# Inverting a 64x64 triangular block on 32x32 diagonal blocks: a DeltaNet and MLP kernel on one core

## The chip, the cores and the metric

The kernel runs on one core of one Trainium2 chip. The metric is the time of one execution on the device in microseconds (us). A core has TensorE (PE: matmuls; PEld: their weight loads, as many as matmuls: 7,158 of each on the page of the kernel before), VectorE (DVE), ScalarE (ACT), GpSimd (POOL) and SyncE (SP, which here only issues DMA transfers). Runs that were marked slow are named as such and left out of the ratios.

## The reference

32 independent heads (4 batches of 8) of 768 steps with head size 48 go through a recurrent "delta rule"; the 8 heads of a batch side by side are the 384 inputs of a two-layer MLP with a tanh-GELU.

```python
k_n = k / (norm(k) + 1e-06)
for t in range(S):                       # S = 768
    y[t]  = q[t] @ state                 # state is 48 x 48 per head
    v_old = k_n[t] @ state
    state = state + beta[t] * outer(k_n[t], v[t] - v_old)
x = y as rows of 384 (8 heads x 48)
h = x @ w_in                             # 384 x 2048
out = gelu_tanh(h) @ w_out               # 2048 x 384
```

The kernel takes 64 steps at a time (a chunk; 12 of them). Inside a chunk the recurrence is a triangular system: with N the masked, beta-scaled product K K^T (64x64 per head), it needs the inverse of I + N. Once that inverse is there, a chunk is a handful of small matmuls per head, and only the state goes from chunk to chunk.

## The kernel before

Every operation is recorded with a cost, the names it reads and writes and a priority; a scheduler in the kernel file then puts them into a fixed order for each engine. So the order that runs is not the order of the source. Heads are handled in pairs: `a` is the head of the pair (upper or lower 64 partitions), `p` the pair (16), `g` half of the pairs (8). The inverse is a Newton iteration on the whole 64x64 block, five rounds of two products and two evictions (copies out of PSUM, where the products of this kernel are written):

```python
def prod(hx, lhs, rhs):                      # 16 matmuls of 64x64x64
    def body():
        return [(bank(hx)[64 * a:64 * a + 64, 64 * p:64 * p + 64], lhs[64 * a:64 * a + 64, p, :],
                 rhs[64 * a:64 * a + 64, p, :], True, True, True) for p in range(8) for a in range(2)]
    return f_mms(body)
...
op(mm_pe(16, 64), {"pe": tr_w}, ...)         # W = I + N transposed on TensorE, 16 transposes
op({"act": 0.6}, {"act": f_act(X[:, :, :], bankb)}, ...)
for j in range(5):
    op(mm_pe(16, 64), {"pe": prod(h1, Zo, X)}, ...)
    op(d_ps(512), {"dve": f_tt(F[:, :, :], bc(twoI), v1(h1), ALU.subtract)}, ...)   # F = 2I - Z'X
    op(mm_pe(16, 64), {"pe": prod(h2, F, Zo)}, ...)
    op(d_act(512), {"act": f_act(dst, v1(h2))}, ...)                                # next Z
```

K and Q are transposed by a DMA transpose per chunk (`KQT`). A chunk's outputs come out with time on the partitions (`x`), and a second DMA transpose (`xT`) turns them for the MLP:

```python
op({"sp": 1.1}, {"sp": f_dma(KQT[i]..., KQ[i]..., True)}, ...)                  # per chunk
op({"sp": 1.1}, {"sp": f_dma(xT[:, s, :, 0:n], x[0:n, s, :, :]..., True)}, ...) # per MLP tile
```

## Time and profile before

| | before |
|---|---|
| median of the first three runs | 323.46 us (323.24 to 327.57) |
| span of the profiled run | 322.0 us |
| TensorE busy | 272.2 us, 85% |
| TensorE waits marked "issue" | 12.7 us |
| instruction packets | 56 of 16 KB |

These lines are from the page of the kernel before: busy us (share of the span) and number of instructions of each engine; busy tenths of TensorE in 40 equal slices and the clock granted to it in tenths; and the DMA queue that carries instructions (packets, MB, share of the engines' span).

```profile
PE 272.2 (85%) x7158; PEld 178.4 (55%) x7158; DVE 175.0 (54%) x279; ACT 175.3 (54%) x309; POOL 127.1 (39%) x96
...
PE   1158745988859789999899979989999999989995
...
PEclk9998775779998799999999999999999999999999
...
q8 instruction: 56, 0.92, 1.2%
```

TensorE is the bound from the 15th slice on. This line of the wait view of the kernel before says how long TensorE stood with nothing to wait for that the profile shows ("issue"): total us, number of times, longest.

```profile
PE ps L301 <- issue: 12.7, 12, 4.0
```

The two MLP layers' matmuls are these groups of the kernel before (count, then busy us and mean ns of one, then idle us before them):

```profile
L301 PE MATMUL ps<-xT,W 128*128 128x512 bf16 (+1 forms) x336 | 80.6, 364 | 1.8 <-ACT gT L294 1.0 <-DMA xT<-x 0.7
L301 PE MATMUL ps<-W,gT 128*128 128x384 bf16 x384 | 70.0, 327 | 0.6 <-ACT gT L294 0.6
```

And this is the timeline of TensorE in the middle of the kernel before: start us, us, form, count.

```profile
128.10 0.44 PE L301 MATMUL ps<-Z,F 64*64 64x64 bf16 x16
128.38 0.67 PE L301 MATMUL ps<-X,Z 64*64 64x64 bf16 x32
128.98 0.82 PE L301 MATMUL ps<-xT,W 128*128 128x512 bf16 x3
```

### The profile page before, as it was taken

To read this page: it belongs to the slowest core of one execution; us is meant where nothing else is said; L and a number is where in the kernel's file an instruction comes from. 1 tells how busy PE (TensorE), PEld (TensorE's weight loads), DVE (VectorE), ACT (ScalarE), POOL (GpSimd) and SP (SyncE) were. 2 spreads that over 40 slices of the span, in tenths; PEclk is the share of its full clock that TensorE was granted. 3 is DMA by queue.
4 is the path that set the end of the run, shared out by engine and by line. 5 is a ranking of instruction groups with operands and counts; after the bars stand their busy time and mean duration, and the time that the engine had idled before them with its cause. 6 is when DMAs were issued, how large, how long until landed. Compare 5 with 4: busy or idle time off the path is not lost.

```text
span 322.0 us, 15234 instructions
## 1 busy us (share of the span) xinstructions
PE 272.2 (85%) x7158; PEld 178.4 (55%) x7158; DVE 175.0 (54%) x279; ACT 175.3 (54%) x309; POOL 127.1 (39%) x96
## 2 busy tenths in 40 slices
PE   1158745988859789999899979989999999989995
PEld 1147644656636466666556556555566556544662
DVE  3489723767557467766775566674556554320111
ACT  4325543668447578634778443777345774168330
POOL 2842330877987257455546371260202211000000
PEclk9998775779998799999999999999999999999999
DMA  7998889879998435495557541709001002101022
GB/s 134 168 182 169 131 119 180 155 151 172 170 176 139 93 69 102 85 181 111 111 100 107 113 103 51 118 4 118 26 29 53 2 9 48 66 36 24 24 75 49
DMA packets 116206, 31.84 MB, mean 99 GB/s; under 512 B 110640, under 2 KB 115760, under 8 KB 116144
## 3 DMA queue, kind: packets, MB, share of 16 engines
q1 hardware_dynamic: 113600, 27.73, 45.5%
q0 software_dynamic: 2544, 3.15, 6.8%
q8 instruction: 56, 0.92, 1.2%
q14 instruction: 6, 0.05, 0.0%
HBM read 20.64 MB, written 4.72 MB: 79 GB/s over the span
## 4 chain that ended last, share of the span: by engine, by line
PE 51%; DMA 22%; issue 7%; DVE 7%; ACT 5%; SPq 4%; POOL 2%; POOLq 0%
PE ps L301 50%; DMA kf<-in_k_dram 8%; DMA qf<-in_q_dram 6%; DMA vf<-in_v_dram 4%; SPq L309 4%; DMA xT<-x 2%; DVE F L285 2%; DMA KQT<-KQ 1%; ACT Z L294 1%; ACT sq L294 1%; ACT x L294 1%; PE ps L600 1%; POOL sr L285 1%; DVE ss L503 1%; DVE R L285 1%
## 5 line engine op out<-in xcount | busy, mean ns | idle before, releaser
L285 DVE TENSOR_TENSOR F<-twoI,ps 128x512 bf16<-128x512 bf16 x120 | 80.4, 684 | 58.4 <-PE ps L301 57.7
L301 PE MATMUL ps<-xT,W 128*128 128x512 bf16 (+1 forms) x336 | 80.6, 364 | 1.8 <-ACT gT L294 1.0
L294 ACT ACTIVATE Z<-ps 128x512 bf16<-128x512 f32 x96 | 56.2, 595 | 42.3 <-PE ps L301 41.5
L294 ACT ACTIVATE gT<-ps 128x512 bf16<-128x512 f32 (+1 forms) x112 | 58.2, 536 | 32.3 <-PE ps L301 31.2
L301 PE MATMUL ps<-W,gT 128*128 128x384 bf16 x384 | 70.0, 327 | 0.6 <-ACT gT L294 0.6
L301 PE MATMUL ps<-X,Z 64*64 64x64 bf16 x1920 | 53.9, 201 | 12.8 <-ACT Z L294 6.9
L301 PE MATMUL ps<-Z,F 64*64 64x64 bf16 x1920 | 54.7, 201 | 8.7 <-DVE F L285 4.0
L301 PEld LDWEIGHTS ps<-X,Z 64*64 64x64 bf16 x1920 | 42.8, 116 | 29.8 <-ACT Z L294 15.1
L301 PEld LDWEIGHTS ps<-Z,F 64*64 64x64 bf16 x1920 | 43.0, 115 | 28.7 <-DVE F L285 15.8
L285 POOL TENSOR_TENSOR W<-identB,N 128x512 bf16<-128x512 bf16 x20 | 23.0, 1151 | 81.8 <-DVE N L285 78.1
L301 PEld LDWEIGHTS ps<-W,gT 128*128 128x128 bf16 x384 | 34.5, 98 | 21.8 <-ACT gT L294 0.8
L301 PEld LDWEIGHTS ps<-xT,W 128*128 128x128 bf16 x336 | 26.7, 100 | 23.1 <-ACT gT L294 4.2
L290 DVE COPY osb<-ps 128x384 f32<-128x384 f32 x20 | 11.1, 557 | 41.3 <-PE ps L301 41.3
L285 POOL TENSOR_TENSOR sr<-ss,half 128x16 f32<-128x16 f32 x9 | 26.2, 2911 | 5.4 <-DVE ss L503 5.2
L285 POOL TENSOR_TENSOR KQ<-kf,rn 128x768 bf16<-128x768 f32 (+1 forms) x12 | 17.1, 1423 | 21.2 <-PE ps L301 16.9
L285 POOL TENSOR_TENSOR NU<-mU,bcol 128x1024 f32<-128x1024 f32 x12 | 23.6, 1971 | 4.4 <-DVE N L285 4.0
L294 ACT ACTIVATE x<-ps 64x768 bf16<-64x768 f32 x24 | 19.3, 804 | 8.2 <-PE ps L301 7.9
L285 POOL TENSOR_TENSOR Z<-identB,N 128x512 bf16<-128x512 bf16 x20 | 23.0, 1151 | 0.0
L294 ACT ACTIVATE TT<-ps 128x512 bf16<-128x512 f32 x24 | 14.3, 596 | 13.4 <-PE ps L301 13.4
L294 ACT ACTIVATE X<-ps 128x512 bf16<-128x512 bf16 x24 | 14.3, 595 | 12.9 <-PE ps L600 12.9
L285 DVE TENSOR_TENSOR N<-ps,NU 128x512 bf16<-128x512 f32 x24 | 16.3, 686 | 8.6 <-PE ps L301 8.6
L301 PE MATMUL ps<-KQT 48*64 48x128 bf16 x384 | 12.7, 246 | 6.6 <-DMA KQT<-KQ 6.4
(49 smaller groups left out, 202.4 us busy)
## 6 DMA issues: line engine op xcount, KB each, us to landing
kf<-in_k_dram SPq DMA_DIRECT2D x24, 192.0 KB, 4.0
qf<-in_q_dram SPq DMA_DIRECT2D x24, 192.0 KB, 3.9
vf<-in_v_dram SPq DMA_DIRECT2D x24, 192.0 KB, 4.3
out_dram<-osb SPq DMA_DIRECT2D x20, 192.0 KB, 1.9
W<-in_moe_w_in_dram POOLq DMA_DIRECT2D x3, 512.0 KB, 6.0
W<-in_moe_w_out_dram POOLq DMA_DIRECT2D x4, 384.0 KB, 7.1
out_dram<-osb SPq DMA_DIRECT2D x8, 96.0 KB, 2.7
BL<-in_beta_dram SPq DMA_DIRECT2D x2, 96.0 KB, 3.6
```

Source lines behind the costliest of these rows:

```text
L285: return lambda e: e.tensor_tensor(out() if callable(out) else out, a() if callable(a) else a, b() if callable(b) else b, op)
L290: return lambda e: e.tensor_copy(out, a() if callable(a) else a)
L294: return lambda e: e.activation(out, a() if callable(a) else a, func)
L301: ins = t.matmul(out, lhsT, rhs, start=st, stop=sp_, skip_group_check=skip)
L309: return lambda e: e.dma_start(out, a)
L503: op({"dve": 0.95 * w}, {"dve": lambda e, u=u: e.tensor_reduce(ss[j][:, u], sq[j][:, u, :], AX.X, ALU.add)}, reads=[f"sq{j}{n}"], writes=[ ...
L600: ins = t.transpose(bankb()[r, p, :], W[r, p, :], identB[r, :])
```

## The change

The intent: only the two 32x32 diagonal blocks of each 64x64 block are inverted by Newton, which takes four rounds, not five, and 32 columns per product, not 64; one merge step then makes the off-diagonal block. The evictions get half as wide. In numbers of matmuls per chunk: 8 products of 64 matmuls of 32x32, and 96 for the merge, in place of 20 products of 16 and 32 transposes. Five more things are in the same change: W is no longer transposed on TensorE (VectorE transposes N); the Gram products (K K^T and Q K^T of a chunk) are cut into smaller matmuls; the outputs are made with time along the free dimension, so the MLP needs no DMA transpose, but six small SBUF-to-SBUF copies per tile and weights loaded in row groups; K and Q of the first three chunks are transposed on TensorE; and the scheduler keeps TensorE on MLP products for 1.2 us at a time.

```diff
-            for j in range(5):
-                op(mm_pe(16, 64), {"pe": prod(h1, Zo, X)}, ...)
-                ...
+            def prod(h, lhs, rhs):                       # 64 matmuls of 32x32x32
+                    for n, p in enumerate(range(ps_.start, ps_.stop)):
+                        for b in BLK:                    # four blocks of 32 partitions
+                            r.append((bank(h)[b, 32 * n:32 * n + 32], lhs(b, p), rhs(b, p), True, True, True))
+            for st in range(4):
+                op(cp, {"pe": prod(h1, cmp_(src), cmp_(X))}, mode="n", ...)
+                op(d_ps(w), {"dve": f_tt(F..., bc(twoI, n_p), view(h1), ALU.subtract)}, ...)
+                op(cp, {"pe": prod(h2, cmp_(F), cmp_(src))}, mode="n", ...)
+                ...
+            op(..., {"pe": f_mms(hm)}, mode="t", ...)    # merge: 32 matmuls
+            op(..., {"pe": f_mms(tm)}, mode="t", ...)    # merge: 64 matmuls
... (Gram products: 48 matmuls per half, in place of 16)
-            op({"sp": 1.1}, {"sp": f_dma(xT[:, s, :, 0:n], x[0:n, s, :, :]..., True)}, ...)
+            for c_ in range(2):
+                for j in range(KT):
+                    op({"sp": 0.5}, {"sp": f_dma(xs[64 * c_ + 48:64 * c_ + 64, j, :, 0:n], xs[...])}, ...)
... (K/Q transposes of chunks 0 to 2 on TensorE)
+                    if e == "pe" and pe_mode == "m" and o.mode != "m" and burst < BURST:   # BURST = 1.2
+                        pr += 5000.0
```

In all TensorE has 11,043 matmuls in place of 7,155; each is two instructions, the weight load and the matmul. (The pages count 11,046 and 7,158, three more each.)

## The prediction

> **What bounds the kernel now.** The profile's page shows TensorE busy 272 of 322 us (85%); VectorE and ScalarE are at 54%, GpSimd 39%. From about 120 us (busy time in 20 us windows) TensorE is busy 18.2 to 19.9 of every 20 us at full clock: it is the bound. Before that it idles 39 us, the DMA engines are about 90% busy to 100 us, and the granted clock falls to 0.59 between 40 and 60 us.
>
> **TensorE now (timeline and group views, from 130 us).** A 64x64 product on two diagonal tiles starts every 17.6 ns, so a batch of 16 takes 0.28 us; products on four tiles start every 8.3 ns. A chunk spends 20x0.28 on Newton, 2x0.28 on transposing W, 0.7 on the Gram products, 1.9 on the state: 8.7 us, 105 us over 12 chunks. The MLP needs about 124 us (0.216 us per 512-column matmul, 0.1625 per 384). Each change between MLP and small products costs 95 ns more than the normal spacing (309 against 216 ns, 125 against 28); the instruction order has 224: 21 us.[...]
>
> **After.** Per chunk: 8 products of 64 32x32 matmuls. Not in this trace; if four tiles start together every ~26 ns (the four-tile groups here show 31 at 48 columns), one is ~0.42 us. Merge ~1.0, Gram 0.8, state 1.65 (the output product now uses four tiles): 6.9 us, 83 us in all. So TensorE saves only ~22 us of work, though VectorE's F evictions fall from 80 to ~33 us, ScalarE loses ~40, GpSimd ~25; mostly off the critical path. PE transposes of chunks 0 to 2 add ~3 us. MLP/small changes fall to 134 (-8.6 us)[...].
>
> **Early phase.** The first Gram waits for the DMA transpose (10.2 to 15.0 us in the chain): on TensorE plus an eviction about 2.5 us sooner. The transpose also holds SyncE's queue 3 to 5 us each; the first MLP tile's transpose is only issued at 49.3 and lands at 56.8 us. Six small copies instead (0.6 us issue each) should start the MLP at 42 to 46 us. I count ~13 us less idle, ~4 us less cold clock.
>
> **New cost.** TensorE instructions grow from 7,155 to 11,043 matmuls. The wait view already has 12.7 us of TensorE "issue" waits. Instruction packets in the trace are 16 KB, ~1.1 us each.[...] Fetch may limit dense stretches: I add ~4 us, perhaps 15.
>
> **Sum.** -22 -8.6 +3 +3.6 (work) -13 -4 (early) +4 (fetch) ≈ -37, on 323.5: about 285 us. Range 269 to 300. Chances: faster by over 2% 0.96, within 2% 0.03, slower 0.01.
>
> **Right if:** 32x32 batches of 64 span ~0.42 us between batch starts; TensorE busy ~235-245 us and still the bound after 100 us; first MLP matmul before 47 us; F evictions ~33 us; idle before 120 us near 25 us.
>
> **Wrong if:** the 32x32 matmuls don't overlap four-fold; "issue" waits on TensorE exceed 25 us; the new serial chain (full-width steps, not two interleaved halves) leaves TensorE waiting on evictions after 120 us; the row-split first-layer weights land later than the first tile is ready; or the early phase gains much more than counted (then under 270).

The sum is -22 -8.6 +3 +3.6 -13 -4 +4 = -37.0 us. The ~26 ns under "After" is an estimate from the 31 ns that stand beside it, and so is the ~0.42 us made of it; the other times of new work there are estimates too, for which the text gives no working. The 4 us of fetch is an estimate beside the 12.7 us of issue waits and the 1.1 us of a packet; how it follows from them is not said. The "3 to 5 us" of SyncE are 3.2 to 4.7 us for the six transposes issued up to 80.2 us, and 1.2 to 4.7 us for all 19.

## More of the kernel before

The start times of the 56 instruction packets are in the trace. The four shortest distances from one to the next are 3.30, 3.62, 3.66 and 3.68 us; none is shorter. The packets are of 16 KB each and take 0.88 to 1.81 us, and the 56 of them go with 14,316 TensorE instructions (7,158 weight loads and 7,158 matmuls): 256 for each packet.

## The result, and the profile after

The changed kernel takes 416.96 us (412.89 to 419.55, 4 runs, one of them slow); the kernel before, 325.27 us in the same rounds. The ratio is 1.278 (95% interval 1.265 to 1.291): 28% slower, where 12% faster was predicted. A ratio here and below is the mean time of one kernel's fast runs over that of the other's of the same rounds, so it is not quite the ratio of the medians.

The same lines of the page, of the changed kernel:

```profile
PE 298.8 (72%) x11046; PEld 190.1 (46%) x11046; DVE 143.4 (34%) x250; ACT 137.5 (33%) x229; POOL 106.0 (25%) x82
...
PE   1336446996475596888886679779655497999996
...
PEclk9999997559557668599866885989765569999999
...
q8 instruction: 86, 1.41, 1.4%
```

VectorE, ScalarE and GpSimd did get lighter, as intended. TensorE has 27 us more busy time and 118 us in which it is not busy, in place of 50. The wait view of the changed kernel names the reason for most of that:

```profile
PE ps L311 <- issue: 86.6, 49, 4.4
```

It is 74 us more than before. And the MLP matmuls, whose number and size did not change, take 21.7 us longer (172.3 in place of 150.6), by the groups of the changed kernel:

```profile
L311 PE MATMUL ps<-x,W 128*128 128x512 bf16 (+1 forms) x336 | 89.3, 414 | 4.4 <-DMA x<-x 2.5
L311 PE MATMUL ps<-W,gT 128*128 128x384 bf16 x384 | 83.0, 372 | 1.8 <-issue 1.8
```

What an issue wait looks like is best seen in the chain that ended last. This is a stretch of it in the changed kernel: start us, us, what (count of matmuls).

```profile
316.35 2.46 issue
318.81 1.26 PE ps L311 x101
320.08 2.32 issue
322.40 1.24 PE ps L311 x121
323.64 2.23 issue
325.87 1.95 PE ps L311 x117
327.82 1.62 issue
329.44 1.40 PE ps L311 x114
330.84 2.35 issue
```

A sawtooth: 1.2 to 2 us of matmuls, then 1.6 to 2.5 us of nothing, with a period of about 3.6 us. Most counts are a little under 128 (the chain view puts a few matmuls on other steps). Counting all TensorE instructions in the trace, weight loads too, between the ends of these stalls gives 256 almost everywhere: the stalls from 305 to 331 us begin at the instructions 17857, 18113, 18625, 18881, 19137, 19393 and 19649. All differences are 256 or 512. A packet of the instruction queue starts 0.1 to 0.7 us before each of these stalls (for example at 308.74, 316.12, 319.93 and 323.52 us) and TensorE goes on 1.3 to 1.5 us after it has landed. In the whole trace all 49 issue waits begin at such a place, and so do 11 of the 12 in the kernel before, whose Newton matmuls are 64x64: the stalls go with the count of instructions, and not with 32x32 tiles as such.

So the reading is: instructions come in blocks of 256 (a packet of 16 KB for each, so 64 bytes per instruction), and in the train above a block is entered 3.5 to 3.8 us after the one before it (for example at 318.81, 322.40, 325.87, 329.44 and 333.19 us). A Newton product of 64 matmuls is 128 instructions and about half a microsecond of work (7.5 to 8.5 ns per matmul in this trace), so a block of such products is used up in a little over 1 us.

The second loss goes with the first. In this train of stalls TensorE's granted clock falls to half (0.50 from 320 to 340 us). These are two lines of the changed kernel's timeline,

```profile
94.62 1.47 PE L311 MATMUL ps<-W,gT 128*128 128x384 bf16 x8
...
311.61 2.74 PE L311 MATMUL ps<-W,gT 128*128 128x384 bf16 x8
```

where eight such matmuls take 1.47 us after 6.7 us without a stall (at 94.62 us) and 2.74 us in the train of stalls (at 311.61 us). From one of these matmuls to the next it is 163 ns at 94.62 us and 320 ns at 311.61 us. By the clock records of the two traces, half clock was granted for 157 us of the span in the changed kernel and for 36 us before; one stretch of it, 34 us long, starts at 307.2 us and covers the rest of this train, in which stalls of about 2.3 us have about 1.2 us of small matmuls between them.

### The profile page after: what moved, and what is told of

Its sections match the earlier page's. It is cut to its first block, busy times and chain, and to the rows that moved or that the text cites. A ratio compares the mean times of both kernels' runs of the same rounds, so it can differ in the third digit from the quotient of the medians.

```text
span 416.6 us, 22911 instructions
## 1 busy us (share of the span) xinstructions
PE 298.8 (72%) x11046; PEld 190.1 (46%) x11046; DVE 143.4 (34%) x250; ACT 137.5 (33%) x229; POOL 106.0 (25%) x82
## 4 chain that ended last, share of the span: by engine, by line
PE 68%; issue 20%; DVE 5%; SPq 2%; ACT 2%; DMA 2%
PE ps L311 66%; SPq L319 2%; PE ps L599 1%; DMA x<-x 1%; DMA BL<-in_beta_dram 1%; DVE F L295 1%; DVE DT L653 1%; ACT Z L304 1%; DVE X L295 1%; ACT TT L304 1%; DVE U L295 0%; DVE KQ L295 0%; DVE NT L667 0%; DVE KQT L300 0%; DVE N L295 0%
## 5 line engine op out<-in xcount | busy, mean ns | idle before, releaser
L311 PE MATMUL ps<-x,W 128*128 128x512 bf16 (+1 forms) x336 | 89.3, 414 | 4.4 <-DMA x<-x 2.5
L311 PE MATMUL ps<-Z,F 32*32 32x32 bf16 x2688 | 34.7, 183 | 32.5 <-issue 27.8
L295 DVE TENSOR_TENSOR F<-twoI,ps 128x512 bf16<-128x512 bf16 (+1 forms) x39 | 25.0, 645 | 76.7 <-PE ps L311 76.6
L311 PEld LDWEIGHTS ps<-x,W 128*128 128x128 bf16 x336 | 32.2, 110 | 41.1 <-issue 12.4
L304 ACT ACTIVATE Z<-ps 128x512 bf16<-128x512 f32 (+1 forms) x39 | 21.9, 564 | 79.7 <-PE ps L311 79.6
L311 PEld LDWEIGHTS ps<-Z,F 32*32 32x32 bf16 x2688 | 28.7, 94 | 38.2 <-issue 31.4
L311 PE MATMUL ps<-X,Z 32*32 32x32 bf16 x2304 | 26.5, 183 | 25.8 <-issue 24.2
L311 PEld LDWEIGHTS ps<-X,Z 32*32 32x32 bf16 x2304 | 21.5, 94 | 33.0 <-issue 26.9
L295 POOL TENSOR_TENSOR NU<-mN,bcol 128x1024 f32<-128x1024 f32 x12 | 23.1, 1929 | 11.8 <-DVE N L295 11.6
L311 PE MATMUL ps<-KQT 48*32 48x64 bf16 (+1 forms) x1152 | 16.3, 233 | 13.6 <-issue 10.9
```

Of the source, the lines that this page charges most:

```text
L295: return lambda e: e.tensor_tensor(out() if callable(out) else out, a() if callable(a) else a, b() if callable(b) else b, op)
L304: return lambda e: e.activation(out, a() if callable(a) else a, func)
L311: ins = t.matmul(out, lhsT, rhs, start=st, stop=sp_, skip_group_check=skip)
```

## The experiments

The theory, A: the supply of instructions. Its rivals: B, one of the other parts of the change (transposed outputs, copies, weight loads, ordering) costs the time; C, the serial chain of full-width evictions, or the changes between tile shapes (95 ns each between MLP and small products, by the prediction's reading of the trace; the expectations call this time drains), holds TensorE, and "issue" is only how that shows.

### 1. The old inverse in the changed kernel

```diff
-                gram(c, g)
-            if c == 0: inverse(c, slice(0, 8), "a"); inverse(c, slice(8, 16), "b")
-            else:      inverse(c, slice(0, NP), "w")
+                intra(c, g)          # 64x64 Newton and Gram products of the kernel before
```

> The changed kernel with the old 64x64 Newton inverse and old Gram products put back; everything else of the change stays. Theory A (instruction supply[...]): 7,203 matmuls again, 57 blocks, TensorE issue waits back under 20 us, time 300 to 320 us. Rival B (the transposed outputs, the six small copies, the split weight loads or the new ordering cost the time): stays above 380 us.

(The trace of the changed kernel: the shortest distance between packet starts there is 3.24 us.)

It takes 321.53 us (320.15 to 324.12); the kernel before, 325.61 us. Ratio 0.988 (0.979 to 0.996). The wait view of this run:

```profile
PE ps L311 <- issue: 7.6, 30, 1.8
```

and of its page:

```profile
q8 instruction: 56, 0.92, 1.2%
```

All of the loss goes with the inverse; rival B falls. It also shows that everything else in the change together is worth about 1.2%, not the 6 to 7% that the prediction gave to it (-8.6 +3 -13 -4, about -23 us; some 4 us less for this kernel, whose order has 172 changes between MLP and small products and not 134).

### 2. The new inverse alone

The kernel before with only masks, Gram products and inverse taken from the changed one.

> The kernel before with only its inverse and Gram products exchanged for the new 32x32 ones; transposes, outputs, weight loads and ordering rules as before. Theory A: 10,995 matmuls, about 86 blocks, TensorE issue waits of 70 to 110 us in a train of 256-instruction steps, time 390 to 430 us. Rival B: 300 to 330 us.

It takes 438.63 us, ratio 1.347 (1.338 to 1.355). Of its wait view:

```profile
PE ps L301 <- issue: 94.6, 60, 5.2
```

and of its page:

```profile
q8 instruction: 86, 1.41, 1.4%
```

The inverse does it alone. That it is even slower than the whole change (1.278) suggests that the other parts help more when TensorE is being starved; which of them was not followed up.

### 3. Half of the Newton matmuls left out

```diff
                     for n, p in enumerate(range(ps_.start, ps_.stop)):
+                        if p % 2:
+                            continue
                         for b in BLK:
```

The result is wrong. All evictions, dependences and tile shapes are as in the changed kernel.

> The changed kernel with every second matmul of the eight Newton products left out (wrong result on purpose); evictions, their sizes, the order of dependences and the tile shapes stay. It has 7,971 matmuls, about 62 blocks. Theory A: issue waits under 30 us, time 310 to 345 us, though the left-out array work is only about 20 us. Rival C (the serial chain of full-width evictions, or drains between tile shapes, holds TensorE): 395 us or more, 417 less at most the 20 us of array work.

It takes 332.35 us (2 runs), 85 us less than the changed kernel. The array work left out is about 23 us by estimate (3,072 matmuls at the 7.5 ns from one to the next in the changed kernel's trace, from 96.02 to 96.50 us); the 20 us of the expectation is an estimate without its working. The issue waits are higher than expected, but fell by 40 us, and the clock came back in part (0.892 on average, 0.811 in the changed kernel, 0.945 before). Of its wait view:

```profile
PE ps L311 <- issue: 46.9, 53, 3.2
```

and of its page:

```profile
q8 instruction: 62, 1.02, 1.3%
```

Rival C falls: the chain was left as it was, and the time went. 62 blocks are six more than before, yet the issue waits are nearly four times as long (46.9 against 12.7 us). The reading is that this kernel's Newton stretches are still denser than the old ones, and that the number of instructions in a stretch against the stretch's length counts, not the total alone; the density was not counted in this run.

### 4. Extra instructions without array work: a miss

```diff
+            for _ in range(2):
+                t.sem_inc(SPARE)      # a semaphore that nobody reads
             ins = t.matmul(out, lhsT, rhs, ...)
```

> The kernel before with two instructions that do no array work (an increment of a spare semaphore) put ahead of each of the 3,840 Newton matmuls: 7,680 more TensorE instructions, as many blocks as the changed kernel has, with all arithmetic and dependences of before. Theory A: about 86 blocks, stalls at every 256th instruction in the Newton stretches, 370 to 420 us. Rivals B and C: 325 to 335 us. If the increments themselves are slow, the matmuls of a batch are spaced evenly wider and no stall stands at the ends of blocks.

It takes 1,363.82 us. The increments are slow: from one Newton matmul to the next, with two increments between, the median is 302 ns (from 702.88 us on, for example, 16 of them take 4.79 us), where the kernel before takes 17.6 ns, so about 140 ns each. As a dose of instructions this is worthless, as the last sentence of the expectation allowed for. One thing may be taken from it: it has 86 instruction packets, as many as the changed kernel, and no issue wait longer than 0.3 us, since they are spread over 1,362 us.

### 5. The disputed cost by itself

The kernel before, then 2,048 matmuls of 32x32 on the four diagonal tiles, in one stream after everything else has ended:

```diff
+            for n in range(512):
+                for r in range(4):
+                    b_ = slice(32 * r, 32 * r + 32)
+                    t.matmul(psum[b_, 0, c_], KQ[0][b_, 0, n % 16, 0:32], KQ[0][b_, 1, n % 16, 0:32], ...)
```

> The kernel before, followed by 2,048 more 32x32 matmuls (4,096 instructions, 16 blocks) on the four diagonal tiles in one stream, waiting for nothing once it starts: the disputed cost by itself. Theory A: the stream runs in steps of 256 instructions, 3.3 to 3.8 us each, 53 to 61 us in all, and the kernel ends 50 to 58 us later. If 32x32 matmuls were slow by themselves, they would be evenly spaced.[...]

(The time of the stream without any limit: at the 7.5 ns measured in the changed kernel it would be about 15 us, an estimate.)

The kernel takes 380.09 us, 52 us more than the one before on the same chip (328.37). The timeline of TensorE in the stream:

```profile
323.34 2.14 PE L794 MATMUL ps<-KQ 32*32 32x32 bf16 x206 [0.65 <-DVE osb L294]
327.49 1.21 PE L794 MATMUL ps<-KQ 32*32 32x32 bf16 x128 [2.00 <-issue]
330.94 1.23 PE L794 MATMUL ps<-KQ 32*32 32x32 bf16 x128 [2.25 <-issue]
334.68 1.23 PE L794 MATMUL ps<-KQ 32*32 32x32 bf16 x128 [2.51 <-issue]
338.69 1.23 PE L794 MATMUL ps<-KQ 32*32 32x32 bf16 x128 [2.78 <-issue]
...
375.87 1.22 PE L794 MATMUL ps<-KQ 32*32 32x32 bf16 x128 [2.52 <-issue]
379.89 0.57 PE L794 MATMUL ps<-KQ 32*32 32x32 bf16 x50 [2.80 <-issue]
```

After the start nothing waits for data here, and the DMA engines are nearly idle (4% busy). The stream still stops after every 128 matmuls. From 327.49 to 379.89 there are 14 steps: 3.74 us for each 256 instructions, or 29 ns per matmul with its weight load. The array itself needs 1.04 us per step, mostly at half clock (8.1 ns per matmul; 0.55 was granted on average from 322 us on). The rest can be followed in the trace: in each of these steps the next packet starts 1.0 to 1.7 us after the first matmul of the block in use and takes about 1 us, and TensorE goes on 1.2 to 1.6 us after it has landed. (In the changed kernel's trace a packet takes 0.88 to 1.65 us, and each of the 49 issue waits ends 1.2 to 1.6 us after one has landed.) So a block cost 3.74 us in this stream, the whole round trip, and not only the transfer of about 1 us.

That gives an estimate of the bound, which the prediction should have made. TensorE's instructions over 256, times the 3.74 us of this stream: 56 x 3.74 = 209 us before, under the 322 us it took; 86 x 3.74 = 322 us after, which is already more than the predicted 285 us, even if the small matmuls had been spread evenly over the whole kernel. They are not, and it took 417. (With the 3.3 to 3.7 us that the trace of before showed by itself the estimate is 284 to 316 us, so even then the forecast of 285 us had no room.)

### 6. The first experiment once more

> Placeholder for a second look at the changed kernel with the 64x64 inverse (same file as the first experiment) beside the following runs: 318 to 324 us, issue waits 5 to 15 us on TensorE.

322.72 us in one run, beside 328.37 us: a repeat, no more.

### 7. The early phase alone

The kernel before, with K and Q of the first three chunks transposed on TensorE (eight transposes per half chunk and one eviction), all else as it was.

> The kernel before with only the transposes of the first three K/Q chunks moved to TensorE. If the early phase is worth what the prediction gave it, 6 to 13 us less (310 to 318 us). If early gains are given back later (TensorE is the bound from 120 us on only as long as chunk work arrives), under 4 us less (321 to 326 us).

329.97 us, ratio 1.003 (0.995 to 1.012): nothing. The chunk chain does start earlier (TensorE is busy 6.2 us of the first 20 us, 3.35 before), but the first MLP matmul comes at 55.5 us, 56.8 before, and this is what the 200 us from 120 us on look like, first in the kernel before, then in this one (stretch, its length, then busy us of TensorE, PEld, VectorE and so on):

```profile
120.00:320.00 200.00, 191.15 (x4605) 117.71 (x4598) 102.24 (x155) 111.77 (x199) 59.45 (x43) 1.00 0.34 70
```

```profile
120.00:320.00 200.00, 185.76 (x4708) 116.63 (x4707) 101.88 (x153) 110.67 (x198) 63.69 (x46) 0.99 0.37 71
```

Up to 120 us TensorE has 2.7 us more busy time than before (83.8 and 81.0), and in this stretch 5.4 us less: what is won at the start is idle time later. The issue waits rose from 12.7 to 17.9 us, which may be part of it; the rest was not settled.

### 8. Fewer instructions by other algebra

If small TensorE instructions are what costs, the 384 transposes of W can go: with K scaled by the root of beta, the Gram matrix is symmetric, so I + N^T is read from the same PSUM bank with the other mask. The scale then sits in V too, and U needs none.

```diff
-            op({"pe": tr_w}), op({"act": f_act(X, bankb)})                     # transpose W, evict to X
+            op(d_ps(512), {"dve": f_tt(pv(W), gview(0), bc42(mL), ALU.mult)})  # N^T: lower mask
+            op(d_pool(512), {"pool": f_tt(X, bc64(I64), W, ALU.add)})
+            rnb = rn * sqrt(beta)        # K scaled; V scaled by sqrt(beta); U = copy of T'R
```

It stands on the kernel of the first experiment.

> The changed kernel with the 64x64 inverse, and K scaled by the root of beta, so that the Gram matrix is symmetric and the transposed start of the iteration is read from it: 768 fewer TensorE instructions in weights and matmuls (6,819 matmuls), no transposes of W on TensorE, 14 us less on ScalarE, 16 us more on VectorE. If fewer small TensorE instructions are what pays: 6 to 14 us under the first experiment, 308 to 316 us. If the dependence chain or the DMA limits it: within 3 us of the first experiment.

314.84 us (313.48 to 318.09), ratio 0.961 (0.951 to 0.972): the fastest version, and the only one clearly faster than the kernel before. It computes the right result. But it is no gain in the supply of instructions: its issue waits, 10.6 us, are not below the 7.8 us of experiment 6, the kernel without this edit on the same chip. TensorE is busy 267.7 us in place of 273.0 there; what the rest of the gain is made of was not taken apart. Of its page:

```profile
PE 267.7 (85%) x6822; PEld 177.6 (57%) x6822; DVE 190.3 (61%) x313; ACT 162.9 (52%) x287; POOL 125.0 (40%) x103
```

and of its wait view:

```profile
PE ps L311 <- issue: 10.6, 10, 2.0
```

### 9 and 10. Without the new ordering rule

`BURST = 0.0` in place of `1.2`, in the kernels of experiments 1 and 8.

> The changed kernel with the 64x64 inverse, and without the new ordering rule that keeps TensorE on MLP products for 1.2 us at a time: 204 changes between MLP and small products instead of 172, so 3 us more of drains at 95 ns each. If that is all: 322 to 327 us. If the rule costs more than it saves, because it makes the chunk chain wait (TensorE idle from 120 us on was 9 us in the kernel before and about 22 us in the first experiment): 312 to 319 us.

Four runs, two of them slow (326.57 and 328.41); the two fast ones are 319.85 and 321.40 us. Beside 326.22 us for the kernel before this is no different from experiment 1. It is inconclusive.

> The kernel with K scaled by the root of beta, without the new ordering rule: 214 changes instead of 170, 4 us more of drains. If that is all: 316 to 321 us. If the rule costs more than it saves: 305 to 313 us.

319.32 us, ratio 0.982 (0.973 to 0.992), 0.961 with the rule. So nothing says that the rule holds the chunk chain up; here it seems to help, by 4.5 us between the medians, about the 4 us expected of fewer changes at 95 ns each. The two intervals almost touch, so the size is uncertain.

### 11. The other algebra without the change

The edit of experiment 8 in the kernel before.

> The kernel before with only K scaled by the root of beta, so that the transposed start comes from the symmetric Gram matrix: 384 fewer TensorE transposes (768 instructions with their weight loads), nothing of the change under study. If the gain of the scaled version (ratio 0.961) is its own: 0.965 to 0.98 of the kernel before, about 313 to 319 us. If it came from the parts of the change that it was built on: 0.985 to 1.0.

321.04 us, ratio 0.993 (0.984 to 1.002; one of four runs slow). So neither part does much alone (0.988 and 0.993), and together they give 0.961. The product of the two is 0.981; the intervals are about 0.01 wide on each side, so whether they really help each other stays open.

## Why the prediction was wrong

- **"TensorE saves only ~22 us of work", with a product of 64 at ~0.42 us.** As array time this was close: without the stalls a product takes 0.48 us (the 64 matmuls from 96.02 to 96.50 us of the changed kernel's timeline, 7.5 ns each), and 8.1 ns each, mostly at half clock, in experiment 5. It was the wrong quantity. In the stream of experiment 5 each 256 instructions took 3.74 us, 3.6 times the 1.04 us of their array time.
- **"Fetch may limit dense stretches: I add ~4 us, perhaps 15."** This is the step that failed: the mechanism was named, and its size was off by a factor of about 18. It is 74 us of issue waits, five times even the "perhaps 15". Numbers enough to see it coming were in the trace of before: the smallest distance between instruction packets (3.3 to 3.7 us) and the number of instructions (14,316 in 56 packets). The prediction counted only with the 1.1 us that a packet is in transfer; two of its products, 256 instructions, are about 0.85 us of work by its own estimate. In experiment 5 the time from entering a block to entering the next, 3.74 us, is more than three times the transfer.
- **"~4 us less cold clock".** The sign was wrong. With the stalls the granted clock fell from 0.945 to 0.811 on average (with fewer of them it is 0.892 in experiment 3 and 0.936 in experiment 1), and the MLP matmuls, which had nothing to do with the change, took 21.7 us more. 74 and 22 are 96 us, and the profiled spans differ by 94.6 us; the small sum of everything else has not been taken apart.
- **"~13 us less idle" early, first MLP matmul at 42 to 46 us.** It came at 62.3 us, and idle time before 120 us was 53 us, not 25. Without the new inverse (experiment 1) it came at 50.3 us, and the early stretch did gain: TensorE was busy 87.8 us of the first 120 us, 81.0 before. But this kernel is only 1.2% faster. The early gain is idle time again later; the wait view shows 7.6 us of TensorE waiting for the six small copies there, 0.7 us for the DMA transposes before. This and experiment 7 suggest that early idle time counts only if the work that it pulls forward is what runs out at the end; no run tests that by itself.
- **Changes between MLP and small products, -8.6 us.** They fell to 134 in the order, as said. Nothing of it could be seen behind the stalls.
- **Evictions.** The F evictions fell from 80.4 to about 33 us (22.5, 7.5, 2.5 and 0.8 us by form), exactly as predicted, and it was worth nothing: they were off the critical path.
- Of the reasons given for being wrong, "issue waits on TensorE exceed 25 us" was the true one. The serial chain (experiment 3) and the late weights (experiment 1) were not. The probability given to "slower", 1%, was far too low for a change that adds 54% more instructions to the busiest engine.

## What to carry to other kernels

Count the instructions of the busiest engine and divide by the block that its queue is fed with: on TensorE in experiment 5, 256 instructions (128 matmuls with their weight loads) per 3.74 us, 29 ns per matmul; no other engine's queue was measured. A tiling that makes matmuls shorter than that on average over a block gained nothing here, however well it packed the array (7.5 to 8.1 ns per matmul within a block); the fewer, larger matmuls of the old inverse were faster although they multiply zeros (321.53 us in experiment 1, 416.96 us in the changed kernel). The train of stalls on TensorE was paid twice here, because the granted clock fell too (0.811 on average, 0.945 before); and the trace of the old kernel shows the limit already, in the shortest distances between instruction packets (3.3 to 3.7 us).
